# One core, attention then an MLP mixer: a new order for every engine's instructions, omega's load ahead of k's, buffers given to the longest free

## The chip, the cores and the metric

The kernel runs on one core of a Trainium2 chip. The metric is device time in microseconds (us). All times of before come from three timed runs and from one profiled execution. The engines are TensorE (PE, with its weight loads PEld), VectorE (DVE), ScalarE (ACT), GpSimd (POOL) and SyncE (SP). Each takes its instructions strictly in the order in which the program issues them to it. SP, POOL and ACT also issue DMAs.

## The reference

Eight batches, 8 heads, 576 rows, head size 64, 128 random features. What is computed, cut to its core:

```python
def phi(x):                                     # x scaled by 64 ** -0.25
    h = einsum('bhsd,md->bhsm', x, omega) - sum(x * x, -1) / 2
    return exp(h - max(h, -1)) / sqrt(128)
kv  = einsum('bhsm,bhsd->bhmd', phi(k), v)      # per head: 128 x 64
z   = sum(phi(k), axis=2)
x   = (phi(q) @ kv) / (phi(q) @ z + 1e-6)       # heads side by side: 8 x 576 x 512
u   = x + (relu(x.T @ w_tok1) @ w_tok2).T       # token mix, 576 -> 256 -> 576
out = u + relu(u @ w_ch1) @ w_ch2               # channel mix, 512 -> 1536 -> 512
```

## The kernel before

**Stages.** Every batch b goes through three functions. `attention` makes the features of q and k by matmuls with omega (`kp` L650, `qp` L666) and exponentials on ACT (L515); takes, per row of k, the largest feature (`km` L678, a reduce and a reciprocal on DVE) and scales v with it (`vs_` L687, usually POOL); sums over rows into kv (`kv` L697), copies that out (`kv_out`), multiplies with q's features (`num` L728) and divides (`num_out` L740, a reciprocal and a multiply on DVE). `token_mix` is two matmul layers (`t1`, `t2`), a relu, and `uadd` on DVE; the result u is transposed by a DMA of SP's queue (`ut_dma`) into uT. `channel_mix` has 12 first-layer jobs per batch (`c1`, L967, four matmuls of 512 columns each) with a relu each, then a second layer. The last 64 rows of all batches are gathered and go through `channel_mix` as a ninth batch, c = 8. `token_mix` for batch 0 is a special form with PE transposes.

**The second layer** of batch 0 is plain (`c2`, L1001). That of c = 1 to 8 (`channel_out_fast`, L917) uses seven products of half size instead of eight; for this it needs, per batch, eight sums of half blocks of the first layer's result (`go` at L877, S in the trace, two groups of four), differences of the weights (T, L448, four on DVE once), and reads that add the products to u and to each other (L906, DVE). The helper for the sums, L295, has one choice:

```python
def tt(eng, **kw):
    (nc.gpsimd if eng == "POOL" else nc.vector).tensor_tensor(**kw)
```

**What sets the order.** All work is first collected as 1211 jobs, numbered as they are added. `Planner.run` then issues them in the order of the list ORDER. A negative entry issues a warm-up matmul on zeros (L1039) into a bank. Every engine runs its part of that list in that order, and each job waits for the jobs it depends on. The dictionary MOVED replaces the usual engine of a job (`engine` is asked where the job is added). SLOT gives, one digit each, the ring buffer or PSUM bank (8 banks) that a job takes at its first use; the list may only name one whose earlier owner's readers have all been issued.

```python
for tag, name in j.take:
    if (tag, name) not in self.held:
        i = self.held[tag, name] = int(next(slots))
```

**Loads.** q, k and v of batches 0 and 1 come by POOL's DMA queue in their natural layout and are transposed on PE; only k of batch 0 comes by four loads of SP and ACT (L385), and omega by SP (L395). From batch 2 on, POOL's queue casts q and k to a scratch in DRAM (L359, L364, L370), and SP transposes them back (`back` L380: qT, kT). The weights w_ch1 (wc1, L425) and w_ch2 (wc2, L440) come in two halves each by POOL's queue.

**Job numbers used below.** 2: omega's load. 3, 5 (ACT) and 4, 6 (SP): k of batch 0. 7: the tail rows of k, batch 0 (POOL). 0: identities (POOL). 38 to 40: omega scaled, transposed, copied. 41, 44: PE transposes of k, batch 0. 47, 48, 67 to 70: the path of k's tail rows. 137, 141, 145, 149: the four copies of uT, batch 0. 150, 153, 156, ...: first-layer jobs of batch 0. 191: a first `c2`. 329: kT of batch 2; 598, 599: qT and kT of batch 4. 301 to 308, 436 to 442, 571 to 578, ... and 1163 to 1170: the sums S of c = 1, 2, 3, ... and 8. 275, 276 and 545, 546: tail rows' second token layer and its add. 401: a relu of token mix, batch 2, and 402 the `t2` job after it. 584: a read of c = 3, and 586 the product after it. 1129, 1121: last products of c = 7; 1175 to 1197: products of c = 8 (half size). 1199 to 1210: the last stores.

Of the kernel before, what the change touches and what calls it, by code (L numbers as in the profile page):

```python
# [81 lines left out]
]  # L82
SLOT = (
    "0001203450670100531642027046313724005203716031213170242506371243501030126450300623741115037622415010"
    "3157143302010163207240531170360711422336140014632220751302761220105427113005401216030201704522131743"
    "5632010231741610520432015370243105072320714330625120712006304015123156124230220105611334112101502001"
# [985 lines left out]
```

## Time and profile before

| what | value |
| --- | --- |
| three timed runs, median (lowest to highest) | 283.94 us (282.96 to 285.21) |
| profiled execution, first to last instruction (span) | 281.1 us, 2.84 below that median; its own device time is not recorded apart |
| PE busy with matmuls | 270.3 us, 96% |
| DVE / ACT / POOL busy | 222.4 / 138.6 / 92.0 us |
| granted TensorE clock, mean | 0.998 |
| chain that ended last | PE 89%, DVE 3%, DMA 2%, ACT 2% |
| matmul groups on the chain | L967 32%, L917 26% |

A row of the instruction groups reads: line, engine, operation, output<-inputs, shapes, count, then busy time and the mean of one, then the engine's idle time before it. In a time line, `x4` means that four like instructions were merged into one row. A row of the windows gives, for one stretch of the span, the busy time of each engine, the granted clock and the mean busy share of the DMA engines.

### The profile page before, as it was taken

How to read it: one execution, taken by the hardware profiler on the slowest of the kernel's cores; microseconds unless marked ns; L12 is line 12 of the kernel's file. 1: busy time of each engine (PE TensorE's matmuls, PEld its weight loads, DVE VectorE, ACT ScalarE, POOL GpSimd, SP SyncE). 2: the span in 40 equal slices, each digit the busy share in tenths (PEclk: the TensorE clock that was granted, in tenths of full speed). 3: DMA queues.
4: the chain of work that ended last, by engine and by line, in shares of the span. 5: the costliest groups of instructions: out<-in, count | busy, mean ns of one | idle time of the engine just before them, and what ended most of it. 6: DMA issues, size and time to landing. Idle time of an engine off the chain costs nothing.

```text
span 281.1 us, 6278 instructions
## 1 busy us (share of the span) xinstructions
PE 270.3 (96%) x2526; PEld 167.6 (60%) x2526; DVE 222.4 (79%) x462; ACT 138.6 (49%) x288; POOL 92.0 (33%) x116
## 2 busy tenths in 40 slices
PE   6899999999999999999999999999999999999993
PEld 2547546443657755665667647755676467446782
DVE  2589828499999899996997999977995893565992
ACT  1498994049676418743758445734753510031200
POOL 8574994007510872048008710510033000000001
PEclk9999999999999999999999999999999999999999
DMA  6999999999998999997979993960151304030125
GB/s 161 194 189 161 157 169 213 178 191 202 179 218 184 148 172 186 181 198 104 212 178 185 241 135 101 161 156 2 76 97 59 111 0 96 0 149 2 75 90 135
DMA packets 80524, 39.66 MB, mean 141 GB/s; under 512 B 63984, under 2 KB 76016, under 8 KB 80304
## 3 DMA queue, kind: packets, MB, share of 16 engines
q0 software_dynamic: 31744, 17.74, 44.1%
q1 hardware_dynamic: 46832, 15.77, 29.1%
q10 hardware_dynamic: 1920, 5.77, 5.4%
q8 instruction: 19, 0.31, 0.4%
q14 instruction: 9, 0.07, 0.1%
HBM read 35.95 MB, written 16.52 MB: 187 GB/s over the span
## 4 chain that ended last, share of the span: by engine, by line
PE 89%; DVE 3%; DMA 2%; ACT 2%; issue 0%; SPq 0%; DVEq 0%
PE bank L967 32%; PE bank L917 26%; PE bank L791 5%; PE bank L778 5%; PE bank L1001 4%; PE bank L735 3%; PE bank L657 3%; PE bank L702 3%; DMA wc<-in_k_dram 2%; PE bank L669 2%; ACT kp L515 1%; PE bank L845 1%; PE bank L817 1%; PE bank L737 1%; PE bank L771 1%; DVE T L448 1%
## 5 line engine op out<-in xcount | busy, mean ns | idle before, releaser
L967 PE MATMUL bank<-uT,wc 128*128 128x512 f16 x376 | 89.6, 379 | 0.5 <-DVE r L292 0.4
L290 ACT ACTIVATE r<-bank 128x512 f16<-128x512 f32 (+1 forms) x86 | 47.7, 601 | 82.7 <-PE bank L967 61.5
L295 POOL TENSOR_TENSOR vs<-v,vs 128x512 f16<-128x512 f16 x32 | 34.2, 1072 | 94.4 <-DVE vs L683 51.3
L967 PEld LDWEIGHTS <-wc 128*128 128x128 f16 x424 | 38.8, 98 | 38.8 <-issue 1.6
L917 PEld LDWEIGHTS <-r 128*128 128x128 f16 x384 | 36.8, 98 | 8.2 <-issue 1.1
L515 ACT ACTIVATE kp<-bank 128x512 f16<-128x512 f32 x64 | 36.7, 618 | 8.9 <-PE bank L657 7.1
L515 ACT ACTIVATE qp<-bank 128x512 f16<-128x512 f32 x64 | 36.7, 614 | 8.8 <-PE bank L669 5.8
L681 DVE TENSOR_REDUCE km<-kp 128x8 f16<-128x1024 f16 x32 | 38.7, 1208 | 1.2 <-ACT kp L515 1.1
L292 DVE TENSOR_SCALAR r<-bank 128x512 f16<-128x512 f32 (+1 forms) x40 | 26.3, 670 | 15.7 <-PE bank L967 11.3
L745 DVE TENSOR_TENSOR x<-bank,rc 128x320 f16<-128x320 f32 x62 | 30.5, 492 | 2.1
L917 PEld LDWEIGHTS <-S 128*128 128x128 f16 x288 | 28.1, 98 | 5.8 <-issue 0.3
L906 DVE TENSOR_TENSOR o<-u,bank 128x512 f32<-128x512 f16 x28 | 19.0, 679 | 6.2 <-PE bank L917 5.8
L917 PE MATMUL bank<-T,r 128*128 128x256 f16 x192 | 23.8, 273 | 0.0
L917 PE MATMUL bank<-wc,r 128*128 128x256 f16 x192 | 23.6, 273 | 0.0
L917 PE MATMUL bank<-T,S 128*128 128x256 f16 x192 | 23.4, 273 | 0.0
L946 POOL DMA_DIRECT2D out_dram<-o x2 | 1.3, 645 | 61.2 <-issue 61.2
L906 DVE TENSOR_TENSOR o<-o,bank 128x512 f32<-128x512 f32 (+1 forms) x27 | 16.6, 617 | 2.5 <-PE bank L917 1.8
L735 PEld LDWEIGHTS <-qp 128*128 128x128 f16 x256 | 13.5, 98 | 8.1 <-DVE kvsb L286 0.7
L794 DVE TENSOR_TENSOR u<-x,bank 128x512 f16<-128x512 f16 x28 | 17.6, 680 | 0.0
L735 PE MATMUL bank<-kvsb,qp 128*128 128x65 f16 x256 | 15.0, 193 | 0.5 <-DVE kvsb L286 0.5
L791 PE MATMUL bank<-r,w 128*128 128x512 f16 x56 | 14.1, 381 | 0.0
L744 DVE RECIPROCAL rc<-bank 128x5 f32<-128x5 f32 x62 | 11.4, 184 | 2.9 <-PE bank L737 2.2
(119 smaller groups left out, 379.0 us busy)
## 6 DMA issues: line engine op xcount, KB each, us to landing
out_dram<-o ACTq DMA_DIRECT2D x9, 512.0 KB, 2.7
q<-in_q_dram POOLq DMA_DIRECT2D x6, 576.0 KB, 9.7
wc<-in_moe_w_ch_dram POOLq DMA_DIRECT2D x4, 768.0 KB, 9.0
k<-in_k_dram POOLq DMA_DIRECT2D x6, 512.0 KB, 7.8
v<-in_v_dram POOLq DMA_DIRECT2D x6, 512.0 KB, 9.9
out_dram<-o SPq DMA_DIRECT2D x5, 512.0 KB, 3.9
r<-in_q_dram POOLq DMA_DIRECT2D x4, 288.0 KB, 7.5
v<-in_v_dram POOLq DMA_DIRECT2D x4, 256.0 KB, 8.1
```

The lines of the kernel that those rows point to most:

```text
L290: nc.scalar.activation(out=out, in_=in_, func=AF.Relu)
L292: nc.vector.tensor_relu(out=out, in_=in_)
L295: (nc.gpsimd if eng == "POOL" else nc.vector).tensor_tensor(**kw)
L515: nc.scalar.activation(out=out, in_=in_, func=AF.Exp, bias=0.0, scale=1.0)
L681: nc.vector.reduce_max(out=mx, in_=kpv, axis=AX.X)
L735: nc.tensor.matmul(ps[:, k, j * 65 : (j + 1) * 65], st, s[:, i, 0 : D + 1], start=True, stop=True)
L745: nc.vector.tensor_tensor(out=t_x[place("x", b)][:, :, (2 * hp + hs[0]) * D : (2 * hp + hs[0] + n) * D].rearrange("p j (i d) -> p i j d", ...
L791: nc.tensor.matmul(ps, w2_of(tb, j), r1[:, tb, :], start=(tb == 0), stop=(tb == NT - 1))
L794: nc.vector.tensor_tensor(out=t_u[place("u", b)][:, j, :], in0=t_x[place("x", b)][:, j, :], in1=bank(n), op=ALU.add)
L906: nc.vector.tensor_tensor(out=o, in0=a, in1=ps, op=ALU.add)
L917: nc.tensor.matmul(ps[:, j * DH : (j + 1) * DH], a[:, cb, j * P : (j + 1) * P], w[:, cb, :], start=(bank_of(b, j0) not in held and j == j0 ...
L967: nc.tensor.matmul(ps, wc1[:, db, cb * P : (cb + 1) * P], moving(db), start=(db == 0), stop=(db == ND - 1))
```

## The change

Only the tables ORDER, SLOT and MOVED change; no job is added or taken away, and the functions are the same. There are 23 warm-up matmuls on both sides, 21 instead of 23 of them ahead of the first channel-mix job of batch 0.

- On SP the order of the first loads becomes omega (2), k (4), k (6); before it was 4, 2, 6. On POOL the tail rows of k (7) are issued ahead of the identities (0). The order of POOL's loads among themselves is the same for all of them.
- The path of k's tail rows (47, 48, 67 to 70) and omega's copy (40) go ahead of the transposes of k (41, 44).
- Engines: six `vs_` go from POOL to DVE; `kv_out` is 18 on DVE instead of 14; token mix's relus on DVE 5 instead of 2; copies of transposed rows on DVE 9 instead of 6; first copies of k 1 instead of 2; batch 0's output copies 0 instead of 2; uT copies 2 instead of 3; the copy of k's tail rows 0 instead of 1; the duplicate of q's tail features goes from DVE to POOL; channel relus 35 instead of 36.
- 42 of the 64 sums S carry the letter ACT in the new MOVED; none had an entry before. `tt` puts every letter but POOL on VectorE.
- Stores: SP has 16 instead of 14, ACT 13 instead of 14, POOL 1 instead of 2. Of the last twelve, ACT has seven instead of four and SP four instead of six.
- SLOT: a job takes the ring buffer or bank that has been free for the longest time.

The diff, cut to its head, the stretches that are spoken of, and the tables' first and last lines:

```diff
--- before.py
+++ after.py
@@ -20,87 +20,69 @@
...
 ORDER = [
-    4, 3, 0, 2, 5, 7, 1, 6, 16, 14, 10, 15, 9, 8, 12, 38, 11, -1, -2, -3, -4, -5, -6, -7, -8, 39, 41, 13, 44,
-    42, 21, 40, 47, 45, 48, 76, 22, 46, 77, 67, 43, 68, -4, -6, 120, 18, 105, 78, 107, 82, -3, 49, 71, 106, 122,
...
-    382, 351, 353, 595, 284, 299, 354, 292, 190, 352, 279, 288, 300, 478, 397, 280, 472, 400, 473, 305, 306,
...
-    398, 401, 301, 480, 302, 309, 479, 399, 474, 307, 492, 310, 503, 494, 489, 408, 303, 505, 402, 493, 409,
...
-    636, 623, 550, 663, 569, 664, 453, 624, 570, 622, 745, 571, 773, 746, 667, 572, 670, 566, 573, 747, 575,
...
-    1125, 1127, 1140, 1149, 1128, 1114, 1131, 1150, 1148, 1129, 1132, 1134, 1155, 1162, 1163, 1158, 1130, 1121,
-    1156, 1164, 1167, 1171, 1168, 1165, 1183, 1172, 1173, 1169, 1122, 1175, 1174, 1133, 1179, 1166, 1170, 1181,
-    1180, 1177, 1176, 1182, 1185, 1178, 1199, 1188, 1186, 1187, 1184, 1200, 1189, 1195, 1190, 1193, 1202, 1196,
-    1208, 1207, 1197, 1201, 1194, 1191, 1206, 1205, 1198, 1209, 1210, 1192, 1203, 1204,
...
+3, 7, 2, -1, 5, 4, 0, -2, 6, 10, 1, 9, 8, 12, 38, 39, 11, 40, 16, 13, 47, 48, 21, 67, -7, 68, 22, 41, 70, -2, 42, 43, -3, 14, 69, 76, 90, 18, 78, -8,
+91, 17, -1, 44, 77, 71, -7, 92, 49, 82, -6, 45, 50, 105, 52, 96, 107, 19, 79, 106, -7, 83, 46, -7, -4, 53, 81, 120, 30, 84, 51, 121, 108, 122, 54, 97,
+-7, 109, 93, 111, -5, 94, 72, 28, 74, 55, 110, 98, 85, 112, 95, 57, -2, -4, 73, 123, 126, 56, 219, 75, 80, 61, 20, 99, -3, 221, 63, -8, 88, 125, 127,
...
+466, 367, 349, 284, 394, 293, 288, 350, 597, 368, 301, 351, 353, 595, 478, 396, 294, 289, 596, 480, 354, 302, 275, 352, 290, 492, 397, 305, 506, 400,
+276, 306, 303, 307, 398, 401, 479, 309, 399, 508, 494, 402, 493, 404, 403, 507, 408, 310, 503, 489, 405, 406, 491, 313, 409, 505, 490, 407, 504, 520,
...
+752, 563, 556, 624, 759, 1001, 564, 570, 545, 760, 667, 575, 762, 873, 779, 668, 576, 761, 670, 874, 669, 780, 577, 753, 671, 579, 571, 1006, 764,
+572, 754, 546, 763, 674, 875, 678, 580, 573, 672, 574, 676, 673, 581, 578, 677, 675, 583, 679, 582, 680, 781, 584, 742, 787, 744, 776, 765, 586, 789,
...
+1158, 1145, 1126, 1146, 1159, 1127, 1149, 1128, 1160, 1140, 1114, 1131, 1148, 1150, 1143, 1132, 1129, 1134, 1144, 1121, 1130, 1163, 1167, 1164, 1175,
+1168, 1122, 1169, 1173, 1165, 1133, 1170, 1177, 1174, 1166, 1171, 1181, 1172, 1179, 1182, 1188, 1180, 1176, 1184, 1178, 1189, 1185, 1200, 1199, 1190,
+1183, 1186, 1193, 1187, 1202, 1201, 1191, 1194, 1205, 1195, 1192, 1206, 1203, 1197, 1196, 1204, 1208, 1207, 1198, 1209, 1210,
 ]
 SLOT = (
-    "0001203450670100531642027046313724005203716031213170242506371243501030126450300623741115037622415010"
...
+    "02030450700360511247000362151270643307110622570401711633300542074621031214067201514226317601250301007146135622173305120105743104725336171426"
...
 )
 MOVED = {
-    42: "DVE", 43: "ACT", 45: "ACT", 48: "DVE", 51: "ACT", 53: "ACT", 56: "ACT", 60: "ACT", 62: "ACT", 65:
...
-    "DVE", 1160: "DVE", 1200: "SP", 1205: "ACT", 1206: "SP", 1207: "ACT", 1208: "SP",
+42: "DVE", 43: "ACT", 45: "ACT", 46: "ACT", 50: "ACT", 56: "ACT", 60: "ACT", 114: "ACT", 129: "ACT", 143: "DVE", 147: "DVE", 163: "ACT", 175: "DVE",
+179: "ACT", 184: "ACT", 189: "ACT", 190: "ACT", 194: "ACT", 195: "ACT", 226: "DVE", 240: "DVE", 256: "DVE", 286: "DVE", 292: "DVE", 296: "DVE", 300:
+"DVE", 301: "ACT", 302: "ACT", 304: "ACT", 306: "ACT", 307: "ACT", 308: "ACT", 350: "DVE", 364: "DVE", 378: "DVE", 390: "DVE", 401: "DVE", 416: "DVE",
+422: "DVE", 424: "DVE", 428: "DVE", 436: "ACT", 440: "ACT", 441: "ACT", 526: "DVE", 568: "DVE", 570: "DVE", 571: "ACT", 573: "ACT", 574: "ACT", 576:
+"ACT", 577: "ACT", 578: "ACT", 620: "DVE", 648: "DVE", 671: "DVE", 692: "DVE", 696: "DVE", 702: "DVE", 704: "DVE", 706: "ACT", 707: "ACT", 708: "ACT",
+710: "ACT", 711: "ACT", 768: "DVE", 782: "DVE", 794: "DVE", 805: "DVE", 830: "DVE", 832: "DVE", 834: "DVE", 836: "DVE", 841: "ACT", 842: "ACT", 844:
...
+"ACT", 1134: "ACT", 1140: "DVE", 1144: "DVE", 1150: "DVE", 1154: "DVE", 1158: "DVE", 1163: "ACT", 1164: "ACT", 1166: "ACT", 1168: "ACT", 1169: "ACT",
+1170: "ACT", 1202: "ACT", 1205: "ACT", 1207: "ACT", 1208: "SP",
 }
```

More of the change, by code (lines that the diff above doesn't have):

```diff
@@ L22 @@
 ORDER = [
[59 rows of a table removed]
[42 rows of a table added]
 ]
 SLOT = (
-    "0001203450670100531642027046313724005203716031213170242506371243501030126450300623741115037622415010"
-    "3157143302010163207240531170360711422336140014632220751302761220105427113005401216030201704522131743"
-    "5632010231741610520432015370243105072320714330625120712006304015123156124230220105611334112101502001"
-    "1163320402165140211610176412517304000612037524002145223000117023104325137202120117305042100576141135"
-    "2740507154076110042751603114022705011041315732121403000112045010725110200405061403012301765403706427"
@@ L89 @@
-    "5643015206241073100625101246023220116534201330523111135160224716051246514725364700113516422103135174"
-    "1625317524300060120373642501100433627516043075122761076423700560420017305611117230017341570146002140"
-    "73521450047113602"
+    "02030450700360511247000362151270643307110622570401711633300542074621031214067201514226317601250301007146135622173305120105743104725336171426"
+    "10712254621763051274112000261412006104510112026117520214711306235702431006135041032622057213705210041722650312146325117206300114710223304161"
@@ L92 @@
+    "11232104170132042230015040371110251207314615220074103671465213004706203002032164537203031604501120141271610232002231640574152021362741511740"
+    "61203704560203130317010506007214130175362110015614722302107260203547045304615342260217105324010354200600161103517643020253373611024050223514"
+    "11720413223240156305430050672403130567023322751401612450321206714116000270201510421654020172604256037200560140123701410601357615371603251320"
+    "06571105074611300"
 )
 MOVED = {
-    42: "DVE", 43: "ACT", 45: "ACT", 48: "DVE", 51: "ACT", 53: "ACT", 56: "ACT", 60: "ACT", 62: "ACT", 65:
@@ L95 @@
-    "ACT", 75: "DVE", 129: "ACT", 137: "DVE", 139: "DVE", 141: "DVE", 145: "ACT", 147: "DVE", 163: "ACT", 169:
-    "DVE", 171: "ACT", 175: "DVE", 179: "ACT", 190: "ACT", 194: "ACT", 228: "ACT", 242: "DVE", 256: "DVE", 265:
-    "DVE", 278: "DVE", 280: "DVE", 286: "DVE", 300: "DVE", 324: "ACT", 399: "DVE", 426: "DVE", 428: "DVE", 432:
-    "DVE", 434: "DVE", 484: "DVE", 498: "DVE", 552: "DVE", 556: "DVE", 562: "DVE", 593: "ACT", 594: "ACT", 634:
-    "DVE", 662: "DVE", 690: "DVE", 692: "DVE", 700: "DVE", 702: "DVE", 727: "ACT", 768: "DVE", 796: "DVE", 822:
@@ L100 @@
-    "DVE", 828: "DVE", 830: "DVE", 836: "DVE", 838: "DVE", 863: "ACT", 904: "DVE", 970: "DVE", 997: "ACT", 998:
-    "ACT", 1024: "DVE", 1052: "DVE", 1088: "DVE", 1092: "DVE", 1094: "DVE", 1096: "DVE", 1098: "DVE", 1102:
-    "DVE", 1104: "DVE", 1108: "DVE", 1133: "ACT", 1134: "ACT", 1140: "DVE", 1148: "DVE", 1150: "DVE", 1152:
-    "DVE", 1160: "DVE", 1200: "SP", 1205: "ACT", 1206: "SP", 1207: "ACT", 1208: "SP",
+42: "DVE", 43: "ACT", 45: "ACT", 46: "ACT", 50: "ACT", 56: "ACT", 60: "ACT", 114: "ACT", 129: "ACT", 143: "DVE", 147: "DVE", 163: "ACT", 175: "DVE",
@@ new lines @@
+710: "ACT", 711: "ACT", 768: "DVE", 782: "DVE", 794: "DVE", 805: "DVE", 830: "DVE", 832: "DVE", 834: "DVE", 836: "DVE", 841: "ACT", 842: "ACT", 844:
+"ACT", 846: "ACT", 847: "ACT", 863: "ACT", 864: "ACT", 890: "DVE", 902: "DVE", 904: "DVE", 930: "DVE", 939: "DVE", 952: "DVE", 964: "DVE", 972: "DVE",
+977: "ACT", 978: "ACT", 980: "ACT", 981: "ACT", 982: "ACT", 998: "ACT", 1024: "DVE", 1038: "DVE", 1052: "DVE", 1066: "DVE", 1075: "DVE", 1088: "DVE",
+1090: "DVE", 1092: "DVE", 1096: "DVE", 1100: "DVE", 1104: "DVE", 1110: "DVE", 1111: "ACT", 1113: "ACT", 1114: "ACT", 1115: "ACT", 1116: "ACT", 1117:
```

82 rows, old and new, of the table ORDER are left out of this document.

## The prediction

> **What bounds the kernel now.** I read the engine totals first, then PE's waits after 34 us, then windows (columns: length, busy us of PE, PEld, DVE, ACT, POOL, clock, DMA share, GB/s).
>
> ```profile
> span 281.1 us, 6278 instructions
> PE 270.3 (96%) x2526; PEld 167.6 (60%) x2526; DVE 222.4 (79%) x462; ACT 138.6 (49%) x288; POOL 92.0 (33%) x116
> PE bank L967 <- DVE r L292: 0.4, 1, 0.4
> PE bank L771 <- DVE x L745: 0.3, 1, 0.3
> 0.00:34.00 34.00, 28.69 (x401) 17.52 (x402) 23.18 (x57) 23.21 (x56) 24.41 (x38) 1.00 1.05 172
> 34.00:60.00 26.00, 26.00 (x201) 13.13 (x201) 15.93 (x37) 11.99 (x24) 11.57 (x14) 1.00 1.29 182
> 60.00:85.00 25.00, 24.59 (x239) 12.82 (x239) 24.02 (x46) 19.71 (x41) 9.91 (x12) 1.00 1.12 205
> 85.00:110.00 25.00, 25.00 (x238) 15.94 (x237) 22.44 (x49) 12.46 (x27) 13.01 (x16) 1.00 1.04 168
> 260.00:281.10 21.10, 16.23 (x141) 13.51 (x139) 14.74 (x31) 1.57 (x3) 1.28 (x2) 0.97 0.32 100
> 33.54 1.02 PE bank L967 x4
> 47.68 4.10 PE bank L1001 x19
> 265.73 10.52 PE bank L917 x96
> 276.27 0.42 DVE o L906
> ```
>
> The last four rows are of the chain of waits: PE carries it to 276.25, then a read on DVE and the last stores. The two waits are all PE's waits after 34 us. So the kernel is bound by PE from the first `c1` on (L967, 33.54); three places are left where an order can move time: the head before 33.54, new waits of PE, and the tail. DVE stands close behind: 24.02 of 25 us from 60 to 85, 22.44 of 25 after that. An order that is worse for DVE by a few us at one place shows in PE.
>
> **The change part by part.** Matmul work is 248.8 us on both sides (counted from the list of jobs at 0.216 us per 512 columns, x64 below, and 0.110 per matmul of the products, x96 above), of which 15.3 lie ahead of the first `c1`. Warm-ups are as many. Row-tiled groups of matmuls are 96 instead of 87, all nine more in the head, where PE waits anyway (28.69 of 34): 0.
>
> ```profile
> 238.88 13.81 PE bank L967 x64
> 57.35 2.48 DVE L794 TENSOR_TENSOR u<-x,bank 128x512 f16<-128x512 f16 x4
> 262.55 1.28 DVE L292 TENSOR_SCALAR r<-bank 128x512 f16<-128x512 f32 x2
> 60.65 1.37 DVE L851 TENSOR_TENSOR ut<-x,bank 64x512 f16<-64x512 f16 x2
> 269.72 1.02 DVE L295 TENSOR_TENSOR S<-r,S 128x768 f16<-128x768 f16 x2
> 49.12 0.18 DVE L744 RECIPROCAL rc<-bank 128x5 f32<-128x5 f32 x1
> 49.75 0.18 DVE L744 RECIPROCAL rc<-bank 128x5 f32<-128x5 f32 x1
> 63.08 1.21 DVE L681 TENSOR_REDUCE km<-kp 128x8 f16<-128x1024 f16 x1
> 64.39 0.22 DVE L683 RECIPROCAL vs<-km 128x8 f16<-128x8 f16 x1
> 270.66 0.41 DVE L906 TENSOR_TENSOR o<-ut,bank 128x256 f32<-128x256 f16 x1
> 270.99 0.41 DVE L906 TENSOR_TENSOR o<-o,bank 128x256 f32<-128x256 f32 x1
> L286 DVE CAST kvsb<-bank 128x130 f16<-128x130 f32 x14 | 4.0, 291 | 9.4 <-PE bank L711 5.0 <-PE bank L709 4.4
> L295 POOL TENSOR_TENSOR vs<-v,vs x32: 1051/1056/1480, 14.0 to 212.4; 128x512 f16<-128x512 f16 x32
> L295 DVE TENSOR_TENSOR S<-r x16: 547/551/559, 80.7 to 266.5; 128x768 f16<-128x768 f16 x16
> ```
>
> *DVE's prices, back to back.* Successive instructions overlap by some 0.08, so I take distances between starts: an add, relu or read of 512 elements 0.60 (2.48 for 4; relus 1.28 for 2), half a read 0.33 (270.99 − 270.66), a sum S 0.47 (1.02 for 2 less the overlap), the tail's add 1.2 for its two instructions (1.37), a `num_out` 0.63 (49.75 − 49.12), `km` with its reciprocal 1.4, a `kv_out` 0.2 (0.29 less the overlap).
>
> *Engines.* DVE gains six `vs_`, four `kv_out`, three relus, three row copies, and gives away some copies: 214.4 to 218.5 us of work, +4.1; ACT loses about 1. `vs_` on DVE isn't in the trace. It costs at least 0.34 (S's 0.47 scaled from 768 to 512 elements), at most POOL's 1.06; the nearest is the add of 128x512 at 0.60, which I take. It matters little: none of the three large sums below holds one. By the average alone the +4.1 would cost nothing, as DVE has 281 − 222 = 59 us free. Only places count.
>
> *The sums S.* 42 of 64 carry "ACT", and by `tt` they run on DVE as before. If the list was laid out as though they ran beside DVE, DVE has more between two inputs of PE than PE has matmuls. I check this without assuming it: for every wait of DVE on a matmul, I add up the DVE work listed after it until a result that PE needs, and the matmul work listed between the same two points. In the old list no stretch exceeds PE's work by more than 0.1, which agrees with the two waits above. In the new list:
>
> - c = 1. From the `num` of batch 2, head pair 3: 5 `num_out` 3.15, `kv_out` 0.2, six S 2.8, tail add (276) 1.2, relu 401 0.6 = 7.95. PE meanwhile has, before `t2` (402): 2 `c1` and 2 `t1` 3.46, a product group 1.31, and 3 `num`, 2 `kv`, transposes and 3 `qp` by their columns 2.03 = 6.80. **PE waits 1.15.**
> - c = 3. From the `num` of batch 4, head pair 0: a `num_out` 0.63, eight S 3.76, `km` 1.4, tail add (546) 1.2, nine instructions of 0.60 (two relus, four adds, three reads, the last 584) 5.4 = 12.4. PE before product 586: 4 `t2` 1.73, 2 `t1` and a `c1` 2.59, three product groups 3.93, small ones 2.33 = 10.58. **Wait 1.8.**
> - c = 8. From the last but one product of c = 7: eight S 3.76, two reads 1.2, two half reads 0.66 = 5.62 against a product 1.31 and five half ones at 0.655, 4.59, before 1179. **Wait 1.0.** All eight S stand within 2.0 us of PE's work.
> - Three more of 0.2, 0.2 and 0.4.
>
> Sum +4.75, taken as **+4.8**. The time that a result takes from one engine to the next would add; PE's own losses between groups (after 33.54, 233.5 of matmul work take 242.7 up to 276.25) would take about as much off. If DVE never packs denser than 24.02 in 25, these sums grow by 4%, 26 us of DVE work by 1.0, and by the same count smaller overruns that are now just covered add 1.6: 7.4 in all.
>
> *Head.*
>
> ```profile
> 10.16 0.59 ACT L286 CAST kT<-bank 128x512 f16<-128x512 f32 x1 [6.51 <-PE bank L470]
> 16.00:20.00 4.00, 3.93 (x53) 2.01 (x53) 3.83 (x6) 4.00 (x11) 2.41 (x3) 1.00 1.17 211
> 20.00:22.00 2.00, 1.47 (x22) 0.74 (x22) 1.51 (x5) 2.00 (x6) 1.98 (x3) 1.00 0.68 105
> 30.00:32.00 2.00, 1.75 (x22) 1.19 (x17) 1.57 (x3) 2.00 (x6) 2.00 (x4) 1.00 1.00 97
> L440 POOL DMA_DIRECT2D wc<-in_moe_w_ch_dram x2: 846/862/877, 31.9 to 34.4; - x2
> DMA to landing us min/median/max: 10.3/11.5/12.7
> 53.71 2.71 SPq L380 DMA_TRANSPOSE kT<-k  x1
> kT<-k SPq DMA_TRANSPOSE x6, 6.8
> 90.85 3.73 SPq L380 DMA_TRANSPOSE qT<-q  x1
> 97.75 2.96 SPq L380 DMA_TRANSPOSE kT<-k  x1
> ```
>
> ACT is full from its first copy at 10.16 to 33.54 (windows 16 to 22 and 30 to 32 show it without a gap). With omega first and k's tail path ahead, ACT can start near 8.0, with some 0.9 less before the last uT copy: the first `c1` could stand at 30.5, 3.0 earlier. But what follows hangs on loads that POOL's queue issues in the old order: wc2's second half, issued at 34.4, lands up to 12.7 later at 47.1, and the first `c2` stood at 47.68; batch 2's kT, issued by SP at 53.71, lands at 60.5 (6.8) and its matmuls stood at 60.56. In the new list that matmul comes 0.7 us of work earlier, so a PE ahead of time waits there. The loads themselves gain only where the DMA engines idled: shares 0.68 and 1.00 beside 1.17 to 1.29 elsewhere, an estimate of 0 to 1.4 us, 0.7 taken. Head: +0.6 − 0.7 = **−0.1** (−0.8 to +0.7).
>
> *kT of batch 4.* SP transposes qT at 90.85 for 3.73; kT right behind it lands near 101.4; the new list uses it at a place that PE reached at 100.1 before and will reach about 1 later: **+0.4** (0 to 2).
>
> *Tail.*
>
> ```profile
> 274.74 3.33 ACTq L946 DMA_DIRECT2D out_dram<-o  x4
> 272.11 5.64 SPq L946 DMA_DIRECT2D out_dram<-o  x6
> ```
>
> ACT issued four of the last stores in 3.33 us, 0.83 each, ending at 278.07, SP six. The new list gives ACT seven, the last five behind one another: 0.83 more at the end, partly before the last read: **+0.5** (0.2 to 1.3).
>
> Ring buffers and banks given otherwise: no row of PE's waits is for a buffer, so 0 (one more wait of 0.4 is possible).
>
> Sum: −0.1 + 4.8 + 0.4 + 0.5 = +5.6. On the profiled execution: 281.1 + 5.6 = 286.7; with 2.84 between span and median, **289.5**.
>
> **The rivals.**
>
> - **A, the forecast**: 289.5, 286.8 to 292 by the bounds above.
> - **B, no new waits.** The new list was laid out with true loads, and DVE keeps up because PE too is a little slower than its matmuls everywhere. For it: the old list ran DVE at 24.02 of 25 with one wait of 0.3. Against it: the three sums are exact counts at measured prices. It gives −0.1 + 0.4 + 0.5: 284.7, and 281.1 to 286.8 with a part of the waits.
> - **C, faster: ACT bounds the head, not the loads.** It decides from wc2 landing by 44 and kT by 57.5, that is 3 us earlier; then the first `c1` at 30.5 carries through: 283.94 − 3.0 = 280.9 where DVE keeps up as in B. For it: ACT without a gap up to 33.54. Against it: POOL's order of loads is the same and its queue was busy (24.41 of 34).
> - **D, more waits.** DVE no denser than 24.02 of 25: 7.4 instead of 4.8, 292.1. A second source would be POOL: two of its `vs_` are listed within the eight S of c = 3, one just ahead of those of c = 1, one within those of c = 5. If an S is held by a running `vs_`, up to 1.06 each, that makes up to 4.2 more than A, 293.7. Before speaks against it as far as it goes: none of its S is stretched (547 to 559 ns), and one `vs_` at most (1480 instead of 1056).
>
> The Trainium skill's page "SBUF — State Buffer", section "Who interferes with whom", says that a VectorE instruction with two SBUF inputs and a GpSimd instruction that reads SBUF exclude one another for the whole instruction; S and `vs_` are such a pair. No run here shows it yet. By it the sum would be at D's upper end; I give it no more than half of D.
>
> **How the numbers follow.** A 0.52, B 0.23, C 0.10, D 0.15. The likeliest is A, 289.5. A change of 1% (2.84 us, 281.1 to 286.8) is about what a measurement of this kernel tells from none. Faster by over 1%: C, 0.10. Within: B, 0.23. Slower: A and D, 0.67. The range leaves out C, the lower half of B and the end of D: 283.4 to 294. By the slower cases alone it would be 286.8 to 294.
>
> **What would show it.** Right, if PE's waits list DVE as releaser at the second token layer of batch 2 (L791, on relus, about 1.2), at the products of c = 3 (L917, on reads L906, about 1.8) and of c = 8 (on half reads, about 1.0), and if all 64 S are on DVE. Head: the first L967 near 31, the first L1001 near 47.6, a wait of L657 for kT. Tail: five stores on ACT's queue after the last read. Wrong, if DVE's instructions sit further apart or closer than the prices, if the first L1001 stands near 44.5, or if PE waits for ACT or a load at a place not named here.

## The result and the profile after

The changed kernel takes **293.54 us** (292.8 to 294.4, four runs) against 284.44 us (282.96 to 285.21, four runs) before: **1.0327 times** the time, 95% interval 1.0278 to 1.0376. The profiled execution has a span of 291.0 us against 281.1, so 9.9 us more. Executions that were over 1.5% longer than the fastest of the same kernel, at a lower granted clock in the records, are left out of the times below (three of e3's four, 303.6 to 306.2 us; two of e2's, 292.1 and 296.3; one of e13's, 296.0). The tables are shorter in the new file, so each line number of the functions is 18 lower: L277 is the helper of the sums S, L899 the products, L949 `c1`, L888 the reads.

The page's totals, the chain's shares and PE's waits after 30 us that come to 0.3 or more (in total, times, longest):

```profile
span 291.0 us, 6279 instructions
PE 273.1 (94%) x2526; PEld 167.6 (58%) x2526; DVE 228.3 (78%) x471; ACT 139.2 (48%) x284; POOL 86.5 (30%) x110
PE 70%; DVE 20%; ACT 3%; issue 3%; DMA 2%; DVEq 0%; POOLq 0%
```

```profile
PE bank L899 <- DVE o L888: 1.5, 3, 1.1
PE bank L753 <- DVE x L727: 1.4, 3, 0.7
PE bank L684 <- DVE o L888: 1.0, 1, 1.0
PE bank L639 <- DVE u L776: 0.6, 2, 0.4
PE bank L899 <- DVE S L277: 0.5, 1, 0.5
PE bank L651 <- DMA qT<-q: 0.3, 1, 0.3
PE bank L773 <- DVE r L274: 0.3, 1, 0.3
```

The chain was PE's for 89%; now DVE carries 20% of it. PE waits for DVE at many small places and for hardly anything else. Where the time went is read best in another way: for each trace, the time at which PE has done a given amount of matmul work (counted from the list, as in the prediction). The difference between the two traces changes almost only in steps:

| matmul work done (us) | what PE does there | the difference grows by |
| --- | --- | --- |
| up to 56 | head, and c = 0 | +0.3 |
| 56 to 64 | c = 1, second token layer of batch 2 | +1.65 |
| 72 to 80 | end of c = 1, start of batch 4 | +1.6 |
| 120 to 124 | c = 3 | +3.0 |
| 156 to 160, 168 to 172 | c = 5 | +0.8, +0.9 |
| 240 to 244 | c = 8 | +1.4 |
| all between these | | +0.4 |
| after the last product | last reads and stores | -0.1 |

The windows around three of these places (length, then busy us of PE, PEld, DVE, ACT, POOL), two of them in the time lines of VectorE and POOL, and the shortest, median and longest time in ns of the four kinds of sums:

```profile
76.00:90.00 14.00, 13.09 (x128) 7.18 (x126) 12.62 (x29) 9.05 (x18) 4.56 (x6) 1.00 1.16 184
90.00:103.00 13.00, 12.00 (x129) 8.96 (x126) 12.47 (x23) 7.42 (x16) 7.64 (x9) 1.00 0.87 175
137.00:155.00 18.00, 16.04 (x131) 9.25 (x130) 17.11 (x31) 10.20 (x21) 5.41 (x6) 1.00 0.80 150
```

```profile
96.28 1.84 DVE L277 TENSOR_TENSOR S<-r,S 128x768 f16<-128x768 f16 x2
96.52 1.18 POOL L277 TENSOR_TENSOR vs<-v,vs 128x512 f16<-128x512 f16 x1 [0.39 <-DVE vs L665]
...
142.30 1.21 DVE L663 TENSOR_REDUCE km<-kp 128x8 f16<-128x1024 f16 x1
143.74 0.51 DVE L277 TENSOR_TENSOR r<-r 128x768 f16<-128x768 f16 x1
144.16 1.41 DVE L277 TENSOR_TENSOR S<-S,r 128x768 f16<-128x768 f16 x1
143.98 1.18 POOL L277 TENSOR_TENSOR vs<-v,vs 128x512 f16<-128x512 f16 x1 [2.15 <-DVE vs L665]
```

```profile
L277 DVE TENSOR_TENSOR S<-r x16: 544/556/1141, 78.6 to 275.5; 128x768 f16<-128x768 f16 x16
L277 DVE TENSOR_TENSOR r<-r x16: 505/556/793, 80.3 to 276.5; 128x768 f16<-128x768 f16 x16
L277 DVE TENSOR_TENSOR S<-S,r x16: 546/552/1414, 83.7 to 278.0; 128x768 f16<-128x768 f16 x16
L277 DVE TENSOR_TENSOR S<-r,S x16: 507/551/1412, 96.3 to 279.3; 128x768 f16<-128x768 f16 x16
```

In the last two of these stretches DVE is full (12.47 of 13, 17.11 of 18) while PE loses 1 and 2 us. And the sums aren't all of 0.55 any more: one of 1.41 starts at 144.16 while POOL's `vs_` runs from 143.98 to 145.16, and ends 0.4 after that has ended. Four are longer, by 0.86, 0.86, 0.59 and 0.24, all beside a `vs_`. In before the longest of 64 was 0.56, and none ran beside one. The order puts a `km`, which releases POOL's `vs_`, right ahead of sums.

### The profile page after: what moved, and what is told of

It is laid out like the page before. It is cut to its first block, busy times and chain, and to the rows that moved or that the text cites. A ratio compares the mean times of both kernels' runs of the same rounds, so it can differ in the third digit from the quotient of the medians.

```text
span 291.0 us, 6279 instructions
## 1 busy us (share of the span) xinstructions
PE 273.1 (94%) x2526; PEld 167.6 (58%) x2526; DVE 228.3 (78%) x471; ACT 139.2 (48%) x284; POOL 86.5 (30%) x110
## 4 chain that ended last, share of the span: by engine, by line
PE 70%; DVE 20%; ACT 3%; issue 3%; DMA 2%; DVEq 0%; POOLq 0%
PE bank L949 25%; PE bank L899 20%; DVE S L277 5%; PE bank L773 4%; DVE x L727 3%; PE bank L760 2%; DVE km L663 2%; DVE o L888 2%; PE bank L639 2%; PE bank L983 2%; PE bank L684 2%; PE bank L717 2%; PE bank L651 2%; DVE r L274 2%; DMA r<-in_k_dram 2%
## 5 line engine op out<-in xcount | busy, mean ns | idle before, releaser
L949 PE MATMUL bank<-uT,wc 128*128 128x512 f16 x376 | 89.9, 379 | 0.0
L272 ACT ACTIVATE r<-bank 128x512 f16<-128x512 f32 (+1 forms) x84 | 47.5, 606 | 84.2 <-PE bank L949 60.2
L949 PEld LDWEIGHTS <-wc 128*128 128x128 f16 x424 | 38.9, 98 | 39.8 <-issue 1.3
L277 POOL TENSOR_TENSOR vs<-v,vs 128x512 f16<-128x512 f16 x26 | 28.4, 1097 | 70.7 <-DVE vs L665 31.6
L899 PEld LDWEIGHTS <-r 128*128 128x128 f16 x384 | 37.1, 98 | 8.1 <-issue 1.8
L497 ACT ACTIVATE qp<-bank 128x512 f16<-128x512 f32 x64 | 37.5, 616 | 5.8 <-PE bank L651 5.7
L274 DVE TENSOR_SCALAR r<-bank 128x512 f16<-128x512 f32 (+1 forms) x42 | 27.7, 667 | 11.9 <-PE bank L949 10.1
L727 DVE TENSOR_TENSOR x<-bank,rc 128x320 f16<-128x320 f32 x62 | 30.5, 492 | 2.1
L899 PEld LDWEIGHTS <-S 128*128 128x128 f16 x288 | 27.6, 98 | 7.8 <-issue 1.7
L899 PE MATMUL bank<-T,S 128*128 128x256 f16 x192 | 23.7, 273 | 1.9 <-DVE o L888 1.3
L888 DVE TENSOR_TENSOR o<-u,bank 128x512 f32<-128x512 f16 x28 | 19.1, 684 | 6.3 <-PE bank L899 6.2
L899 PE MATMUL bank<-T,r 128*128 128x256 f16 x192 | 23.7, 273 | 0.2 <-DVE o L888 0.2
L899 PE MATMUL bank<-wc,r 128*128 128x256 f16 x192 | 23.1, 273 | 0.0
L277 POOL TENSOR_TENSOR vbd<-vt,vbd 128x512 f16<-128x512 f16 x6 | 6.3, 1051 | 55.6 <-DVE vbd L576 29.4
L928 POOL DMA_DIRECT2D out_dram<-o x1 | 0.7, 667 | 63.2 <-issue 63.2
L888 DVE TENSOR_TENSOR o<-o,bank 128x512 f32<-128x512 f32 (+1 forms) x27 | 16.5, 622 | 2.0 <-PE bank L899 1.7
L717 PE MATMUL bank<-kvsb,qp 128*128 128x65 f16 x256 | 15.9, 193 | 0.0
L773 PE MATMUL bank<-r,w 128*128 128x512 f16 x56 | 14.8, 381 | 0.5 <-DVE r L274 0.3
```

Source lines behind the costliest of these rows:

```text
L272: nc.scalar.activation(out=out, in_=in_, func=AF.Relu)
L274: nc.vector.tensor_relu(out=out, in_=in_)
L497: nc.scalar.activation(out=out, in_=in_, func=AF.Exp, bias=0.0, scale=1.0)
L717: nc.tensor.matmul(ps[:, k, j * 65 : (j + 1) * 65], st, s[:, i, 0 : D + 1], start=True, stop=True)
L727: nc.vector.tensor_tensor(out=t_x[place("x", b)][:, :, (2 * hp + hs[0]) * D : (2 * hp + hs[0] + n) * D].rearrange("p j (i d) -> p i j d", ...
L773: nc.tensor.matmul(ps, w2_of(tb, j), r1[:, tb, :], start=(tb == 0), stop=(tb == NT - 1))
```

## The experiments

Two theories had to be told apart: that the **place of the sums** on VectorE's list costs the time, and that the **engines** do (4.1 us more work on VectorE). Beside them stood the held sums, the head and the banks.

**Sums moved alone (e1).** Only the 64 sums change places on VectorE's list, c = 3 and c = 8 for example:

```diff
-575 (S), km, 576 (S), 577 (S), relu, 571 (S), 572 (S), tail add, read, 573 (S), 574 (S), add, 578 (S)
+571 (S), relu, 575 (S), 572 (S), km, 576 (S), relu, tail add, 573 (S), read, 577 (S), 4 adds, 2 reads, 574 (S), 578 (S)
-1163, 1167, 1164, 1168 (S), half read, 1169, 1165, 1170 (S), half read, 1166 (S)
+1167, 1163 (S), read, 1164, 1165, 1168, 1169 (S), 3 reads, 1170 (S), 4 reads, 1166 (S)
```

> The changed kernel with only the 64 sums S at other places of VectorE's own list (spread to where the engine has room and no vs_ of POOL runs); every other instruction of every engine stands as in the changed kernel, engines too. Theory (the sums are listed in a bunch, late for a VectorE that has to run all of them): adding the lists up with the traces' durations it gains 4.9 us, about 288.6 us (287 to 289.5). Rival (the other engines' moves and orders cost it, the place of the sums nothing): 293 to 294.

Measured 289.14 us against 284.78 for before beside it, ratio 1.018 (1.013 to 1.023); the changed kernel has 1.033. That is the theory's 288.6, and not the rival. So about 4.4 of the 9.1 us hang on where 64 instructions stand in one engine's list. Held sums (sums that a `vs_` beside them makes longer) were not the reason: that trace still has three of 1.06 to 1.42. Right behind the two longest of them, at c = 2, comes a step of 1.7 that the changed kernel doesn't have. The two largest of PE's waits that are left in it:

```profile
PE bank L661 <- DVE u L798: 1.4, 2, 1.1
PE bank L921 <- DVE o L910: 0.8, 2, 0.6
```

**The sums on ScalarE, as the table says (e2).** The 42 sums labelled ACT copy their first operand there and leave out the addition:

```diff
-tt(e_sum, out=o[:, part], in0=a[:, part], in1=b[:, part], op=op)
+if e_sum == "ACT": nc.scalar.copy(out=o[:, part], in_=a[:, part])
+else: tt(e_sum, out=o[:, part], in0=a[:, part], in1=b[:, part], op=op)
```

> The changed kernel with the 42 sums that carry the letter ACT run as copies on ScalarE (they copy the first operand and leave out the addition), all at the places of the changed list. It does what the letters say. Theory (the list was laid out as though these sums ran beside VectorE): VectorE has 42 x 0.47 = 19.7 us less, the waits at c = 1, 3 and 8 go; ScalarE's copies at about 0.8 each may bring some back: 284 to 290. Rival (VectorE's sums aren't what PE waits for): 293 to 294.

Two executions, 287.4 and 290.8 us, lie 3.3 apart, so the total decides little. PE's waits in its trace after 45 us that come to 0.4 or more:

```profile
PE bank L556 <- DMA kT<-k: 3.5, 1, 3.5
PE bank L795 <- ACT qp L519: 0.6, 1, 0.6
PE bank L974 <- DMA uT<-u: 0.5, 1, 0.5
PE bank L795 <- ACT qpt L519: 0.4, 1, 0.4
```

The waits for reads, sums, adds and relus of DVE at c = 1, 3, 5 and 8 are gone. The count by matmul work says more than the total: up to 112 us of work this trace is 0.3 ahead of before, where the changed kernel's is 3.6 behind. Of the 7.3 that it is behind at the last product, 5.3 come between 112 and 119: a wait of 3.5 for kT, which is new, and behind it 3.4 us (143.3 to 146.7) at a granted clock of 0.51. All the rest comes to 2.0, against 10.1 in the changed kernel. So most of the loss goes with these 42 sums' work on VectorE. That fits a list laid out as though the sums ran beside VectorE, though it doesn't prove what the list's maker reckoned with. e3 shows what the wait for kT is.

**VectorE's whole list made anew (e3), and one instruction put back (e11).** e3 changes the order of all of VectorE's instructions after 50 us and nothing else:

> The changed kernel with VectorE's whole list after 50 us in another order, all other engines' lists as in the changed kernel. Theory (only the order within VectorE is wrong): a gain of 6.3 us or a little more by adding up the lists, 286 to 287.5, still above the kernel before by some 2 for the engines that carry more on VectorE. Rival (too much work on VectorE, or PE's, ScalarE's and the DMAs' orders): above 290.

It took 297.88 us, so the expected 286 to 287.5 is missed. Most of the DVE waits are gone, but one new wait is 6.9 us. Its POOL and SP rows at that place, and the landing of the transposes of kT (min/median/max):

```profile
72.03 1.06 POOL L299 TENSOR_TENSOR vs<-v,vs 128x512 f16<-128x512 f16 x1 [2.38 <-DVE vs L687]
73.03 0.95 POOL L341 DMA_DIRECT2D v<-in_v_dram  x1
73.92 12.71 SPq L384 DMA_TRANSPOSE kT<-k  x1
```

```profile
PE bank L661 <- DMA kT<-k: 6.9, 1, 6.9
DMA to landing us min/median/max: 4.8/7.0/18.5
94.26 2.77 PE L921 MATMUL bank<-T,S 128*128 128x256 f16 x12
```

In e3 a `km` (347) stands five instructions earlier; POOL's `vs_`, which waits for it, runs at 72.03 instead of 75.87 in the changed kernel, and the loads of v, k, q and k behind it on POOL's queue start at 73.03, ahead of SP's transpose of kT at 73.92; in the changed kernel they start at 76.88, 2.0 us behind that transpose. e11 puts this one `km` back:

```diff
-347 (km), 378 (kv_out), 389 (km), 364 (kv_out), 390 (vs_), 382 (num_out), 380 (num_out)
+378 (kv_out), 389 (km), 364 (kv_out), 390 (vs_), 382 (num_out), 347 (km), 380 (num_out)
```

> The kernel of the run with VectorE's whole list made anew (e3, 304.6 us) with one instruction pair put back: km of batch 2, pair 0 (job 347) stands again after the num_out that it followed in the changed kernel, some 4 us later; by VectorE's own work that is worth nothing (adding up the lists, 0.0). Theory (in e3 that early km lets POOL run its vs_ at 72.0 instead of 75.9, POOL then issues v, k and q at 73.0 instead of 76.9, and SP's transpose of kT, issued at 73.9, lands 18.5 us later instead of some 7; PE waits 6.9 for it): the wait goes, 286.5 to 289.5. Rival (the transposes are late for another reason, or the slower clock of that run is its cause): 297 or more.

Measured 289.71 us (288.5 to 290.2), 0.2 above the range expected; the profiled executions are 9.0 apart (286.9 against 295.9), for one instruction pair:

```profile
75.67 1.06 POOL L299 TENSOR_TENSOR vs<-v,vs 128x512 f16<-128x512 f16 x1 [6.03 <-DVE rc L748]
76.68 0.95 POOL L341 DMA_DIRECT2D v<-in_v_dram  x1
73.72 3.82 SPq L384 DMA_TRANSPOSE kT<-k  x1
86.65 1.47 PE L921 MATMUL bank<-T,S 128*128 128x256 f16 x12
```

The transpose issues in 3.82 instead of 12.71 and PE doesn't wait. The wait isn't all that it cost: in e3 PE's granted clock is 0.50 from 90.5 to 97.3, and the same twelve products take 2.77 us instead of 1.47. PE reaches the matmuls of that kT 6.8 later than in e11 and has fallen 9.1 behind by the next row of twelve products, so about 2.3 of the 9.0 are the slower clock that followed the wait. A transpose that issues slowly needn't cost: the changed kernel has one too (kT at 128.45, 10.45 us to issue), and PE doesn't wait for it. e2's new wait has the same form: there POOL issues v at 121.78 and SP's transposes of qT and kT follow at 122.10 and 131.93; in the changed kernel v comes at 125.67, behind qT at 125.25. But e11 isn't faster than e1, which moves the sums alone: the rest of VectorE's order, as it is made here, is worth nothing more, against the 286 to 287.5 that I gave e3 without this collision.

**The engines alone (e4, e5).** e4 is the kernel before with the table MOVED of the changed one; e5 is the changed kernel with the table of before.

> The kernel before, its order and buffers, with only the table MOVED of the changed kernel (six vs_ to VectorE, more kv_out, relus and row copies there, stores elsewhere). Theory that only the places of the sums matter: 284 to 285.5. Rival (4.1 us more work on VectorE costs in itself, at places not made for it): adding up the lists gives +4.2, 288.6 (287 to 290).

> The changed order and buffers with the table MOVED of the kernel before (4.1 us less on VectorE, six vs_ back on POOL). Theory (an order fits only the engines that it was laid out for; the work on VectorE is not what costs): adding up the lists, 4.0 slower than the changed kernel, 297.5 us (295 to 300). Rival (the 4.1 us more on VectorE cost about that much wherever they stand): faster than the changed kernel by 3 to 4, 290 us.

e4: 289.36 us, ratio 1.018 (1.014 to 1.021), +4.6. e5: 299.05 us, ratio 1.053 (1.047 to 1.058), 5.5 slower than the changed kernel although it takes 4.1 us off VectorE. In e4 the rival held, in e5 the theory: either table costs about 5 us under the list that wasn't made for it. In e4 the largest wait is for copies that moved to VectorE and stand there behind other work:

```profile
PE bank L739 <- DVE kvsb L290: 1.7, 2, 1.0
```

**Held sums (e6, e8, e13).** e8 measures the pair by itself; it has no attention and no mixer and stores zeros.

> No attention and no mixer: zeros are stored. VectorE and POOL run, 16 times each, alone and beside one another: a sum of two SBUF operands as S (alone; beside vs_ of POOL; beside a fill of POOL that only writes), an add with one operand in PSUM as u (alone; beside vs_), and vs_ alone. Theory (two SBUF operands on VectorE and a POOL instruction that reads SBUF exclude one another): S beside vs_ takes 1.0 to 1.6 instead of 0.55 us, or vs_ 1.5 instead of 1.06, together about 1.5 us a pair; S beside the fill and the add beside vs_ keep their times. Rival (they only share rate, or not at all): no time changes by more than 0.1.

Groups of that run (16 instructions each, busy us, mean ns):

```profile
L54 DVE TENSOR_TENSOR s_alone<-a,b 128x768 f16<-128x768 f16 x16 | 8.9, 558 | 0.5
L60 DVE TENSOR_TENSOR s_scale<-a,b 128x768 f16<-128x768 f16 x16 | 20.0, 1248 | 0.5
L64 DVE TENSOR_TENSOR s_fill<-a,b 128x768 f16<-128x768 f16 x16 | 8.9, 558 | 0.5
L57 POOL TENSOR_TENSOR vs_alone<-v,sc 128x512 f16<-128x512 f16 x16 | 16.9, 1056 | 1.2
L61 POOL TENSOR_TENSOR vs_sum<-v,sc 128x512 f16<-128x512 f16 x16 | 19.9, 1242 | 1.2
L68 DVE TENSOR_TENSOR u_alone<-a,bank 128x512 f16<-128x512 f16 x16 | 11.0, 687 | 0.5
L71 DVE TENSOR_TENSOR u_scale<-a,bank 128x512 f16<-128x512 f16 x16 | 11.0, 687 | 0.5
...
51.98 20.47 DVE L60 TENSOR_TENSOR s_scale<-a,b 128x768 f16<-128x768 f16 x16
```

A sum beside `vs_` takes 1248 instead of 558 ns, `vs_` 1242 instead of 1056; beside a fill, which only writes, the sum keeps 558, and an add with an operand in PSUM keeps 687 beside `vs_`. So of the three pairs tried, the two engines hold each other up only where VectorE has two SBUF operands and POOL reads SBUF. The Trainium skill's page "SBUF — State Buffer", section "Who interferes with whom", says just this of the pairs, and the trace agrees. It also says that the loser waits for the whole instruction; a pair took 20.47 / 16 = 1.28 us, less than the 1.61 of both one after the other, so in a stream the exclusion isn't complete.

e6 and e13 take held sums out of the changed kernel:

```diff
 e6:  sums 304, 308 / 576, 577 / 844, 848 ahead of the km behind which they stood
 e13: the first two of e6, and the tail's add 546 ahead of sums 571, 572; sum 841 behind the next relu
```

> The changed kernel with six sums moved on VectorE ahead of the km behind which they stood (304 and 308 ahead of km of batch 3, pair 2; 576 and 577 of batch 5, pair 2; 844 and 848 of batch 7, pair 2), so that they no longer run beside the vs_ of POOL which that km starts. Theory (a sum beside vs_ is held until vs_ ends: 0.86, 0.86 and 0.59 us in the changed kernel's trace, all in stretches where PE waits for VectorE): the three long sums go back to 0.55 and the kernel gains 1.5 to 2.3, 291.2 to 292. Rival (they are long for another reason, or the kms that now come later cost as much): 293 to 294.

> As e6, and the two sums that were still held there are helped too: the tail's add (546) goes ahead of the sums 571 and 572 of c = 3, and sum 841 of c = 5 behind the relu that followed it. Theory (each held sum costs PE about what it is held, as the 1.1 us that the kernel gained at c = 2 in e6): a further 0.9 at c = 3 and 0.6 at c = 5, about 2.5 below the changed kernel, 290.5 to 291.5 us. Rival (at c = 3 and c = 5 the bunch costs the same without the hold, since VectorE's other work is late too): no better than e6, 292 to 293.

e6: 292.39 us (291.5 to 295.1, ratio 1.031 (1.026 to 1.036)), e13: 292.36 (291.4 to 293.7, ratio 1.027 (1.023 to 1.032)) against 293.54 (1.028 to 1.038): neither total is clear of the changed kernel's. So the traces have to tell. In e6 sum 308 of c = 1 is no longer held, the wait of 1.0 for a read there is gone, and the trace's difference to before falls from 3.6 to 2.5 at that place: a hold of 0.86 was worth about 1.1 us. At c = 3 another sum (571) ran into a `vs_` (1.15 us), and at c = 5 the held sum is 841, which e6 doesn't move (1.14, as in the changed kernel), so e6 tested one place out of three. In e13 those are free too: of all 64 sums one alone is over 0.6, the 1129 ns of this row, a sum of c = 2 at 116 us:

```profile
L299 DVE TENSOR_TENSOR S<-r x16: 548/556/1129, 78.8 to 276.1; 128x768 f16<-128x768 f16 x16
154.00:156.00 2.00, 2.00 (x12) 1.41 (x10) 0.89 (x4) 0.64 (x2) 0.89 (x1) 0.50 1.04 195
```

Yet at c = 3 the difference of e13's trace grows by 4.1 from 120 to 128 us of work, against 2.8 in the changed kernel. About 1.5 of it is made behind the bunch, where the granted clock is 0.50 (second row, a window of that trace; 1.00 in the changed kernel's). That belongs to this execution: its mean clock is 0.992, and 0.997 to 0.999 in the other four. Up to the first product behind the bunch the difference grows by 2.6 instead of 3.0, so the hold of 0.86, with the tail's add moved too, was worth 0.4 there, and c = 5 cost 0.4 less. The rival of e13 holds in the main at c = 3: without the hold the bunch is still late.

**The head (e7, e12) and the banks (e10).** e7 and e12 begin as the changed kernel and go on as the one before.

> The changed kernel's list with its engines up to the c1 job 150 of batch 0 (omega first, k's tail rows first, and so on), then the rest of the kernel before, its order and its engines. Theory (the head is bound by loads whose order is the same): 284.5, from 283.7 to 285.3. Rival faster (ScalarE, which starts 2 us earlier, carries through): 281.5 to 282.5. Rival slower (part of the loss is made in the head): 286 and more.

> The changed kernel's list and engines up to 39.9 us of matmul work (about 60 us), then the kernel before; the lists differ by five jobs at this place, where the first attempt (e7) cut them 26 jobs apart and lost its 5 us within the head at the seam. Theory (the head is worth nothing either way, since the loads and not ScalarE bound it): at 30 us of matmul work within 0.6 of the kernel before in the trace, 284 to 285.8 in all with up to 1 for the seam on VectorE. Rival faster: 281.5 to 282.5. Rival slower (a loss made in the head): 287 and more.

e7 (289.11 us) says nothing of the head: its difference to before is 5.3 us already at 12 us of matmul work, where the changed kernel's is 0.8, which I put down to the 26 jobs at its seam (the place where the two lists are joined). e12, with a better seam, takes 285.41 against 284.92 for before beside it, ratio 1.002 (0.999 to 1.005): no gain or loss of the head with omega first can be measured. (Its trace is 1.0 behind that of before at 30 us of matmul work, more than the 0.6 expected, but before's profiled execution, 281.1, is shorter than those of the runs beside e12, 281.1 to 284.5. Another 2.4 are lost at 39 to 44 us of work, at the seam, so the total isn't the head's alone.)

> The kernel before with only the PSUM banks given anew, each to the one that has been free for the longest, in the same order and on the same engines. Theory (PE waits for no bank in the kernel before): 284 to 285, no change. Rival (the banks' hand-over costs or gains something in the head): a difference of 1 or more.

e10 took 288.28 us, ratio 1.015 (1.009 to 1.021), against the expectation. The loss is made before 20 us: at 4 us of matmul work its trace is 2.3 behind before, at the end 3.0. A warm-up matmul writes a bank, so the warm-ups had to be given other banks too, and a row of eight of them waits 1.7 us for a bank that ACT still reads. Two rows of before, then the same two of e10:

```profile
13.75 0.44 PE L488 MATMUL bank<-ident,r 64*128 64x64 f16 x18
15.98 1.89 PE L1039 MATMUL bank<-S 128*128 128x512 f16 x8
```

```profile
13.72 0.66 PE L488 MATMUL bank<-ident,r 64*128 64x64 f16 x18
18.27 1.89 PE L1039 MATMUL bank<-S 128*128 128x512 f16 x8 [1.75 <-ACT kp L515]
```

Up to the first of these rows both keep the same time. From it to the row of eight e10 takes 4.55 us instead of 2.23: 1.75 are the wait, and about 0.6 are matmuls at a slower rate, which e10 leaves about 2 us later than before does (the same 18 transposes take 0.44 at 13.75 in before, and not until 16.09 in e10). Whether the slower rate has to do with the banks isn't shown. Another 0.7 are lost later, 0.4 of it at 40 us of work.

## Why the prediction was right or wrong

The sign, the main mechanism and the places of the large steps were right; the time lies inside the range, 4.0 us above the predicted one and 0.5 below its end. What happened is the case D (more waits of VectorE, 292.1 to 293.7), to which I gave 0.15, and not A, which ended at 292. Both things that D named are in the trace: VectorE is no denser than 12.47 of 13 us where it is late, and sums are held. My objection to the second, that no sum of before was stretched, said nothing, since none of them ran beside a `vs_`.

- **What bounds the kernel**: right. PE lost its time on waits for DVE, after the head, and in before DVE had little room from 60 to 85 us. e2, with 42 sums off VectorE, shows it best: without its wait for kT its trace loses 2.0 instead of 10.1.
- **The three large sums**: right in place and order, too small. c = 1: 1.15 predicted, 1.65 measured; c = 3: 1.8 and 3.0; c = 8: 1.0 and 1.4. Together 6.05 instead of 3.95. At c = 3 VectorE's stretch, from the `num_out` at 140.42 to the end of the reads at 154.26, takes 13.8 us, where I had added up 12.4, and that difference of 1.4 is about the 1.2 by which the step came out larger. Every price was that of an instruction alone, and some were low by before's own trace: one sum took 0.86 more beside `vs_`; the tail's add takes 1.4 to the next start and not 1.2; and a sum behind a sum starts 0.58 after it, and not 0.47, in 15 of 39 cases in before. e13 shows that the hold alone isn't the answer, since c = 3 stays late without it. The waits also look otherwise than I said: PE waits 0.3 on a relu at c = 1, and at c = 3 in six pieces for adds, a sum and reads, where I had one wait of 1.8 on a read. Only c = 8 shows its wait as forecast, 1.1 on a half read.
- **"Three more of 0.2, 0.2 and 0.4"**: this is the term that was mis-sized most. The end of c = 1 took 1.6, c = 5 took 1.7. I added up stretches between two waits of DVE as though each began with DVE up to date. At 90 to 103 us it was busy for 12.47 of 13 us behind a stretch that was already late, and one sum was held 0.86 longer; e6 shows that this hold was worth 1.1 of the 1.6.
- **Balance of losses and latencies** ("would take about as much off"): unsupported. The steps came out above the sums everywhere, never below.
- **Engines at +4.1 us "would cost nothing, only places count"**: half right. e4 and e5 show 4.6 and 5.5 for a table under the wrong list. With the sums at better places the changed kernel still loses 4.4 us (e1), of which PE's waits for adds and reads are the visible part. A part is the step of 1.7 at c = 2 in e1's trace; what else these 4.4 hang on stays open: a whole new list for VectorE gets no further (e11), and the old engines make it worse (e5).
- **Head** -0.1 predicted, +0.3 in the trace, nothing in e12: the number was right, but by luck. I had the first first-layer matmul 3 us earlier, at 30.5, and this gain lost again to loads. ACT did start at 6.91 instead of 10.16, but that matmul stood at 34.21 (merged into the row below), later than in before (33.54), and PE waited for no kT:

```profile
34.28 0.75 PE bank L955 x3
```

Up to its last uT copy, at 33.76, ACT was busy for 25.3 us, against 22.7 up to 33.54 in before; I had reckoned with 0.9 less. Nor was it full in before from 10.16 on: it was idle for 0.95 ahead of 13.32. Only the first `c2` stood where I said, at 47.5. Rival C (ACT's start carries through) is out all the same.
- **kT of batch 4** +0.4: no wait for it appeared; PE waited 0.3 for a qT of batch 3 instead, at a place that I hadn't named. The collision was real elsewhere: e3 and e2 lost 6.9 and 3.5 us to such a transpose.
- **Tail** +0.5: wrong, -0.1. ACT issued seven stores, but five of them had begun before the last read:

```profile
286.33 0.42 DVE o L888
282.19 6.03 ACTq L928 DMA_DIRECT2D out_dram<-o  x7
282.18 5.45 SPq L928 DMA_DIRECT2D out_dram<-o  x4
```

ACT's last ends at 288.22, 1.47 after the last read (286.75); before it was 278.07 - 276.69 = 1.38.

- **Banks** at 0: right for the changed kernel as far as PE's waits show, but e10 shows that the same rule on before's order isn't free in the head (its warm-ups wait for a bank).

## What to carry to other kernels

An order is laid out for one set of engines and prices: before believing it, read what the code does with each label, and add up each engine's list between two of its waits against the engine that bounds. Begin each such sum with the lateness left by the stretch ahead, and take the price of an instruction beside what will run next to it. A helper engine that gets ahead also starts its DMAs earlier: look at what they meet (one `km` moved by five places cost 9 us, a quarter of it because PE ran slower after its wait). Before a step of a trace is put down to a cause, look whether the granted clock was the same on both sides.

## What the runs showed of the hardware

- Two SBUF operands on VectorE and a POOL instruction that reads SBUF: 1.28 us a pair, against 0.56 and 1.06 alone; a sum beside a POOL fill, and an add with one operand in PSUM beside a `vs_`, keep their times (e8).
- A DMA transpose issued 0.9 us behind the first of a row of POOL's loads (73.92, the first at 73.03) took 12.71 us to issue and 18.5 to land; issued 3.0 us ahead of the same loads, 3.82 to issue (e11).
- After PE's wait of 6.9 us (e3) the granted clock was 0.50 from 90.5 to 97.3, and after that of 3.5 (e2) 0.51 from 143.3 to 146.7; twelve products took 2.77 us instead of 1.47.
